# One store path less: wq's gradient of the second head block stored as whole 128-partition transfers

## The chip, the cores and the metric

The kernel runs on one core of a Trainium2 chip. The metric is the device time of one execution in microseconds; the time before is the median of three runs, 719.05 us (718.98 to 719.26). One further execution was taken with the hardware profiler and took 718.87 us; its span, from the first to the last instruction, is 717.1 us.

## The reference

The kernel computes a forward and a backward pass of one decode step: one row x of 640 values is normalised (layer norm) and goes through attention with a key and a value cache, and beside it through a gated feed-forward part. The outputs are the forward result and the gradients of x, both caches and all weights.

```python
# one token: D = 640; 32 heads of 128; caches of 8192 rows a head; F = 1728; all bf16
q = (xn @ wq), split into 32 heads
scores = einsum("bhqd,bhkd->bhqk", q, k_cache) * 128 ** -0.5
p = softmax(scores)
o = einsum("bhqk,bhkd->bhqd", p, v_cache)
A = o, heads side by side, @ wo
B = (silu(xn @ w1) * (xn @ w3)) @ w2
out = x + A + B
# and with grad_out: d x, d k_cache, d v_cache, d wq, d wo, d w1, d w3, d w2
```

The bulk is data movement: both caches (32 heads of 2 MB each, twice) are read, and gradients of the same size are written. The profile counts 151.34 MB read and 151.34 MB written. The gradient of wq, the subject here, is an outer product: row d of it is xn[d] times the gradient of q, 640 x 4096 values in bf16.

## The kernel before, in words

**Tiling.** A head's cache of 8192 x 128 values stands in SBUF as 128 partitions of 64 rows each, 16 KB a partition, so a load or store of a head moves 2 MB with one contiguous 16 KB run a partition. Heads are worked off one after another in a loop over h (L745). Four heads make a group g (its qs, do, dq and its part of wo's gradient are made together), and eight heads, two groups, make a block b of wq (GW = 8).

**A head.** DVE multiplies the cache tile by a broadcast vector (L425), PE adds up the products over identity matmuls (L427), softmax and its gradient follow on small tiles, PE makes the weighted sums over the cache (L500), and the outer products that are the caches' gradients are written into ot tiles, most rows by DVE (L451) and eight rows of every half by ACT (L445). Four ot buffers, three K buffers and two V buffers (with some early heads in borrowed tiles) carry the stream.

**Queues.** The order on every engine is written out by hand; the semaphores come from the tile framework. SP issues the loads of K and V (L116, L123) as soon as a buffer comes free, and the last two heads' stores. POOL issues the caches' gradient stores, one of 2 MB per head and cache (L458), and the stores of wq's gradient. ACT issues x, g, the wo loads and stores, and a part of the wq loads. All three queues are carried out by the same 16 DMA engines.

**wq and its gradient.** wq_two holds two blocks of wq, 128 partitions x 5 x 2 x 1024. When a group is done, finish_steps (L366) overwrites the group's part of wq_two with the gradient (L383, on ACT). After the second group of block 0 and of block 1 the block's part is stored in two pieces, WQ_PARTS = (0, 3) and (3, 2): three columns of 1024, then two. The first goes out at once through store_columns (L465), the second after the next ot store on POOL (L459 and L460). A partition's share of a piece is three or two runs of 2 KB. Once landed, the place is loaded anew with a later block of wq (L178). Block 2 and the first group of block 3 are stored late, near the end (L785), and the last group from a tile of its own (L824).

**Dealing.** store_columns issues through sparing (L145), not through one plain DMA. It cuts the 128 partitions into 120 and 8: 120 rows on 15 engines of eight rows each, so that one engine (SPARED = 4 in the kernel's own count) gets none. The 8 rows are a transfer of their own, one row on each of eight engines. `dealt` counts where the next transfer that does not use all 16 engines will begin; turn_lanes (L134) moves that place by a tiny load into lane_pad (5, 11 or 17 rows of a few bytes), which nothing reads. If the count allows, the 8 rows go ahead of the 120. At the end of the loop turn_lanes(0) puts the place back.

For block 0 and for block 1 this gives on POOL: the 120 x 3 x 1024 store, a 17-row load, the 8 x 3 x 1024 store; an ot store; the 8 x 2 x 1024 store, the 120 x 2 x 1024 store, a 17-row load. Block 0 has a 5-row load ahead of that.

Of the kernel before, what the change touches and what calls it, by code (L numbers as in the profile page):

```python
# [21 lines left out]
def kernel(  # L22
# [22 lines left out]
    nc = tc.nc  # L45
# [22 lines left out]
    WIDE = 4  # L68
    LANES = 16
    SPARED = 4  # L70
    assert H % GW == 0 and GW % GH == 0 and 0 < REST < P and P % GH == 0
    scale = float(DH) ** -0.5

# [30 lines left out]
    with tc.manual_schedule(engines=ORDERED):  # L104
# [29 lines left out]
        def turn_lanes(to):  # L134
            k = (to - dealt[0]) % LANES
            if k:
                rows = k if k > 1 else LANES + 1
                nc.gpsimd.dma_start(lane_pad[0:rows, dealt[1] % 2], wq_v[0:rows, 0:2, 0:8])
                dealt[:] = to % LANES, dealt[1] + 1

        def deal(dst, src, p0, p1):
            nc.gpsimd.dma_start(dst[p0:p1], src[p0:p1])
            dealt[0] = (dealt[0] + (LANES - 1 if p0 == 0 else P - p0)) % LANES

        def sparing(dst, src):  # L145
            rows = P - P % (LANES - 1)
            if dealt[0] == (SPARED + 1 + P - rows) % LANES:
                deal(dst, src, rows, P)
                deal(dst, src, 0, rows)
                turn_lanes(SPARED + 1)  # L150
            else:
                turn_lanes(SPARED + 1)
                deal(dst, src, 0, rows)
                turn_lanes(SPARED + 1)
                deal(dst, src, rows, P)

        def store(dst, src, later=False, by=nc.gpsimd.dma_start):
            if later:
                late.append((by, dst, src))
            else:  # L160
                by(dst, src)
# [5 lines left out]
        def wq_part(b, c0, n):  # L167
            cols = slice(b * GW * DH, (b + 1) * GW * DH)
            return wq_two[:, c0:c0 + n, b % 2, :], wq_v[:, c0:c0 + n, cols], dwq_v[:, c0:c0 + n, cols]
# [196 lines left out]
        def finish_steps(g):  # L366
            G_ = grp[g]
            wo_g = G_["wo"]
            on, on_bf = on_cols(g)
            behind_o.append((g, on_bf))  # L370
            yield
            assert not behind_o
            for r in range(GH):
                nc.scalar.activation(wo_g[:, r, :], g_bc_bf[:], ACTF.Copy, scale=on[:, r:r + 1])
            if g == NG - 2:
                store(dwo_v[g], wo_g[:], True)
            else:
                nc.scalar.dma_start(dwo_v[g], wo_g[:])
            yield
            yield  # L380
            b, k = divmod(g, HB)
            for ci in range(NC):
                nc.scalar.activation(G_["wq"][:, ci, :], G_["dqbc"][:].rearrange("p h d -> p (h d)"),  # L383
                                     ACTF.Copy, scale=xn_col[:, ci:ci + 1])
            if g < NG - HB and k == HB - 1:
                if g == NG - HB - 1:
                    part, _, dst = wq_part(b, 0, NC)
                    store(dst, part, True)
                else:
                    columns.extend((b, *part) for part in WQ_PARTS)  # L390
                    store_columns()
            if g >= NG - HB:
                store(dwq_v[:, :, g * GH * DH:(g + 1) * GH * DH], G_["wq"], True)
            grp.pop(g)
# [54 lines left out]
        def outer_v(st, vec, w2, which, h, half, n):  # L449
            j0 = half * JH  # L450
            nc.vector.tensor_tensor(st.ot[half][:, 0:n],  # L451
                                    vec.rearrange("p (a b) -> p a b", b=2).unsqueeze(1).to_broadcast([P, n, DH // 2, 2]),
                                    w2[:, j0:j0 + n, :].unsqueeze(2).to_broadcast([P, n, DH // 2, 2]), ALU.mult)
            dst = {"V": dvc, "K": dkc}[which][h]
            if h >= H - TAIL:
                nc.sync.dma_start(dst[:, j0:j0 + JH, :], st.ot[half].rearrange("p j a b -> p j (a b)"))
            elif half:
                nc.gpsimd.dma_start(dst.rearrange("p j d -> p (j d)"), st.rows[:])  # L458
                if columns:  # L459
                    store_columns()  # L460
# [4 lines left out]
        def store_columns():  # L465
            b, c0, n = columns.pop(0)
            part, _, dst = wq_part(b, c0, n)
            store(dst, part, by=sparing)

        def row_max(st):  # L470
            st.S = small.tile([P, J], F32, name="S_sb", bufs=1)
# [419 lines left out]
```

## Time and profile before

| what | value |
|---|---|
| median of three runs | 719.05 us (718.98 to 719.26) |
| profiled execution, its span | 718.87 us, 717.1 us |
| busy: PE, DVE, ACT, POOL | 557.1, 630.6, 484.2, 49.5 us (78%, 88%, 68%, 7%) |
| moved | 303.32 MB, 423 GB/s in the mean |
| stores of ot on POOL | 60 of 2048 KB, median 24.4 us from issue to landing |
| loads of K and V on SP | 32 and 32 of 2048 KB, median 26.6 and 20.0 us |
| stores of wq_two by the dealt path | 2 x 720, 2 x 48, 2 x 480, 2 x 32 KB |
| loads of lane_pad | 6, of 0.2 to 0.5 KB |

The profile's page gives busy time by engine, the span in 40 slices with the mean busy share of the 16 DMA engines and the rate, the DMA queues (q0 is POOL's, q1 is SP's, q10 is ACT's; q8 and q14 fetch instructions), the chain of work that ended last, the costliest groups of instructions, and the DMA issues with the time from issue to landing. "L458" is line 458 of the kernel. Behind the page stands the trace, which also has every DMA packet with its queue, start, length and size, and the sixteen completion counts of every transfer.

### The profile page before, as it was taken

What the parts mean: (1) busy time and instruction counts of PE and PEld (TensorE: products, weight loads), DVE (VectorE), ACT (ScalarE), POOL (GpSimd) and SP (SyncE); (2) the same over time, 40 slices, a digit from 0 to 9 for tenths busy, and PEclk for the clock granted to TensorE, in tenths of its full rate; (3) what the DMA queues carried; (4) which work ended last, traced back from release to release, by engine and by line L of the source; (5) the groups of instructions that cost most, each with busy time, mean ns of one, the idle gap of its engine ahead of it and who ended that gap; (6) DMA issues with size and microseconds to landing.
All of it is one profiled execution on the core that took longest, in us unless ns stands there. A gap on an engine that the chain in (4) does not pass through costs nothing.

```text
span 717.1 us, 9854 instructions
## 1 busy us (share of the span) xinstructions
PE 557.1 (78%) x3516; PEld 272.4 (38%) x3516; DVE 630.6 (88%) x723; ACT 484.2 (68%) x1472; POOL 49.5 (7%) x91
## 2 busy tenths in 40 slices
PE   6878988878788777776887787488868789877772
PEld 4753443334333333333343344143434334333331
DVE  5789999999989895997899899499999889899982
ACT  1275778796769656694587867468677857777552
POOL 0010000000001110000000110000000000000100
PEclk9698999998989998997899989899999878999995
DMA  9999999999999999999999999999999999999997
GB/s 364 416 425 430 431 430 430 429 429 429 428 432 428 426 428 424 429 427 426 432 431 428 430 422 426 428 430 429 428 428 431 429 430 431 429 430 429 429 421 288
DMA packets 27039, 303.32 MB, mean 423 GB/s; under 512 B 3249, under 2 KB 3959, under 8 KB 9327
## 3 DMA queue, kind: packets, MB, share of 16 engines
q1 hardware_dynamic: 12832, 154.88, 50.9%
q0 software_dynamic: 10960, 137.72, 45.2%
q10 hardware_dynamic: 3198, 10.10, 3.5%
q8 instruction: 27, 0.44, 0.2%
q14 instruction: 22, 0.17, 0.1%
HBM read 151.34 MB, written 151.34 MB: 422 GB/s over the span
## 4 chain that ended last, share of the span: by engine, by line
DMA 45%; DVE 31%; PE 17%; ACT 3%; issue 2%; POOL 0%; ACTq 0%; DVEq 0%; POOLq 0%
DMA Kt<-in_A_k_cache_dram 28%; DVE T L425 15%; DMA out_dram<-ot 12%; DVE ot L451 10%; PE ob L500 4%; DMA lane_pad<-in_A_wq_dram 4%; PE psS L427 3%; PE psDP L427 3%; ACT ot L445 2%; DVE DP_sb L526 1%; DVE S_sb L472 1%; PE dh_ps L591 1%; PE dx_ps L626 1%; PE gate_ps L602 1%; PE ps_od L516 1%
## 5 line engine op out<-in xcount | busy, mean ns | idle before, releaser
L427 PE MATMUL psDP<-T,ident_bf 128*128 128x512 bf16 x512 | 157.0, 462 | 64.6 <-DVE T L425 64.6
L427 PEld LDWEIGHTS <-ident_bf 128*128 128x128 bf16 x1024 | 108.3, 109 | 212.6 <-issue 140.1
L445 ACT ACTIVATE ot<-qs_g,Uf 128x128 bf16<-128x128 bf16 x504 | 154.0, 394 | 45.1 <-DVE Uf L539 27.2
L425 DVE TENSOR_TENSOR T<-Kt,qs_g 128x4096 bf16<-128x4096 bf16 x64 | 146.4, 2287 | 20.0 <-DMA Kt<-in_A_k_cache_dram 18.8
L445 ACT ACTIVATE ot<-do_g,Pf 128x128 bf16<-128x128 bf16 x512 | 156.3, 389 | 6.2 <-DMA out_dram<-ot 5.2
L425 DVE TENSOR_TENSOR T<-Vt,do_g 128x4096 bf16<-128x4096 bf16 x64 | 146.0, 2282 | 3.9 <-DMA Vt<-in_A_v_cache_dram 3.9
L427 PE MATMUL psS<-T,ident_bf 128*128 128x512 bf16 x512 | 129.0, 397 | 17.7 <-DVE T L425 17.7
L451 DVE TENSOR_TENSOR ot<-qs_g,U 128x3072 bf16<-128x3072 bf16 (+2 forms) x64 | 112.6, 1760 | 11.9 <-DMA out_dram<-ot 11.8
L451 DVE TENSOR_TENSOR ot<-do_g,P 128x3072 bf16<-128x3072 bf16 (+2 forms) x64 | 112.3, 1755 | 6.3 <-DMA out_dram<-ot 5.2
L458 POOL DMA_DIRECT2D out_dram<-ot x60 | 32.2, 537 | 549.2 <-DVE Uf L539 303.6
L500 PE MATMUL ob<-Vt,P 128*4 128x512 bf16 x512 | 64.1, 394 | 0.0
L500 PE MATMUL ob<-Kt,U 128*4 128x512 bf16 x512 | 60.5, 379 | 1.4 <-DVE U L533 1.4
L494 ACT ACTIVATE Pf<-E,rZ 128x16 f32<-128x16 f32 (+1 forms) x32 | 9.8, 307 | 60.2 <-DVE rZ L489 60.2
L558 ACT ACTIVATE dq_diag<-ident_bf,odq 128x128 bf16<-128x128 bf16 x32 | 12.8, 401 | 47.8 <-DVE odq L554 47.8
L516 PEld LDWEIGHTS ps_od<-pick,wide 128*128 128x128 f32 x256 | 38.1, 213 | 7.8 <-issue 3.0
L516 PE MATMUL ps_od<-pick,wide 128*128 128x2 f32 x256 | 33.8, 254 | 0.5 <-ACT wide L508 0.5
L500 PEld LDWEIGHTS <-U 128*4 128x4 bf16 x512 | 19.8, 84 | 37.5 <-DVE U L533 6.6
L476 PE MATMUL sm<-ident_f,mrow 128*128 128x128 f32 x64 | 15.9, 331 | 22.3 <-DVE mrow L474 22.3
L500 PEld LDWEIGHTS <-P 128*4 128x4 bf16 x512 | 20.8, 86 | 25.8 <-issue 3.5
L508 ACT COPY wide<-ob 128x256 f32<-128x256 f32 x64 | 20.1, 363 | 12.7 <-PE ob L500 12.7
L472 DVE TENSOR_REDUCE S_sb<-psS 128x64 f32<-128x512 f32 x32 | 21.9, 685 | 5.6 <-PE psS L427 5.6
L317 ACT COPY woT<-ps_t 128x512 bf16<-128x512 bf16 x40 | 22.9, 577 | 4.2 <-PE ps_t L312 3.6
(174 smaller groups left out, 552.4 us busy)
## 6 DMA issues: line engine op xcount, KB each, us to landing
out_dram<-ot POOLq DMA_DIRECT2D x60, 2048.0 KB, 24.4
Kt<-in_A_k_cache_dram SPq DMA_DIRECT2D x32, 2048.0 KB, 26.6
Vt<-in_A_v_cache_dram SPq DMA_DIRECT2D x32, 2048.0 KB, 20.0
out_dram<-ot SPq DMA_DIRECT2D x8, 1024.0 KB, 12.7
out_dram<-wo_g ACTq DMA_DIRECT2D x6, 640.0 KB, 15.1
wo_g<-in_A_wo_dram ACTq DMA_DIRECT2D x6, 640.0 KB, 15.8
wq_two<-in_A_wq_dram SPq DMA_DIRECT2D x1, 2560.0 KB, 23.8
w1t<-in_B_w_dram SPq DMA_DIRECT2D x1, 2160.0 KB
```

The source lines that it names most:

```text
L317: nc.scalar.copy(woT[:], ps_t[:])
L425: nc.vector.tensor_tensor(T[:], src[:, :, ds_], vec[:, ds_].unsqueeze(1).to_broadcast([P, J, DHH]), ALU.mult)
L427: nc.tensor.matmul(ps[:], lhsT=ident_bf[:], rhs=T[:, :, RUN * i:RUN * (i + 1)], start=(half == 0 and i == 0), stop=(half == 1 and i == DHH ...
L445: nc.scalar.activation(st.ot[half][:, JH - n + j].rearrange("p a b -> p (a b)"), vec, ACTF.Copy, scale=wf[:, half, j:j + 1])
L451: nc.vector.tensor_tensor(st.ot[half][:, 0:n], vec.rearrange("p (a b) -> p a b", b=2).unsqueeze(1).to_broadcast([P, n, DH // 2, 2]), w2[:, ...
L458: nc.gpsimd.dma_start(dst.rearrange("p j d -> p (j d)"), st.rows[:])
L472: nc.vector.tensor_reduce(st.S[:], st.ps["S"][:], AX.X, ALU.add)
L476: nc.tensor.matmul(st.sm[:, 8:8 + P], lhsT=mrow[:].to_broadcast([P, P]), rhs=ident_f[:], start=True, stop=True, skip_group_check=True)
L500: nc.tensor.matmul(ob[c0:c0 + WIDE, :], lhsT=w2[:, WIDE * q:WIDE * (q + 1), 0], rhs=src[:, WIDE * q:WIDE * (q + 1), :].rearrange("p j d -> ...
L508: nc.scalar.copy(part[:], ob[:, i * (WIDE // 2) * DH:(i + 1) * (WIDE // 2) * DH])
L516: nc.tensor.matmul(st.od, lhsT=st.wide[i][:, b * DH:(b + 1) * DH], rhs=pick[:, r, :], start=(r == 0), stop=(r == WIDE - 1), skip_group_che ...
L558: nc.scalar.activation(dq_diag[:], ident_bf[:], ACTF.Copy, scale=odq[:, 1:2])
```

## The change

The dealt path is kept for the blocks under SPARING_BLOCKS = 1, so for block 0. Block 1's two pieces are issued as they are, 128 partitions each, by POOL's plain dma_start. With them go the two 8-row stores and the two 17-row loads of block 1. The order on all other engines is the same.

```diff
     SPARED = 4
+    SPARING_BLOCKS = 1
...
         def store_columns():
             b, c0, n = columns.pop(0)
             part, _, dst = wq_part(b, c0, n)
-            store(dst, part, by=sparing)
+            store(dst, part, by=sparing if b < SPARING_BLOCKS else nc.gpsimd.dma_start)
```

On POOL, around the change:

```diff
 out_dram<-ot 128x8192
-out_dram<-wq_two 120x3x1024
-lane_pad<-in_A_wq_dram 17x2x8
-out_dram<-wq_two 8x3x1024
+out_dram<-wq_two 128x3x1024
 out_dram<-ot 128x8192
-out_dram<-wq_two 8x2x1024
-out_dram<-wq_two 120x2x1024
-lane_pad<-in_A_wq_dram 17x2x8
+out_dram<-wq_two 128x2x1024
 out_dram<-ot 128x8192
```

## The prediction

> **What bounds the kernel now.** I read the page's stretch by slices first, then the DMA queues, then a table of busy time by stages, then POOL's own instructions around the change, and last the packet records of the trace. The page:
>
> ```profile
> DMA  9999999999999999999999999999999999999997
> GB/s 364 416 425 430 431 430 430 429 429 429 428 432 428 426 428 424 429 427 426 432 431 428 430 422 426 428 430 429 428 428 431 429 430 431 429 430 429 429 421 288
> q1 hardware_dynamic: 12832, 154.88, 50.9%
> q0 software_dynamic: 10960, 137.72, 45.2%
> q10 hardware_dynamic: 3198, 10.10, 3.5%
> ```
>
> The mean of the 16 DMA engines is busy in every slice but the last, and the rate stays near 430 GB/s. The three queues (SP's q1, POOL's q0, ACT's q10) add up to 99.6% of 16 engines' span. By stages (time, then PE, PEld, DVE, ACT, POOL busy, granted clock, DMA share, GB/s):
>
> ```profile
> 403.00:452.00 49.00, 40.94 (x246) 19.64 (x245) 46.56 (x51) 35.49 (x110) 7.42 (x11) 0.91 1.01 425
> 452.00:470.00 18.00, 7.71 (x37) 3.70 (x35) 8.85 (x7) 6.34 (x21) 0.53 (x1) 0.72 1.02 433
> 470.00:690.00 220.00, 177.03 (x1063) 81.34 (x1064) 205.27 (x225) 160.98 (x502) 13.51 (x24) 0.91 1.01 429
> 690.00:717.10 27.10, 11.09 (x86) 6.91 (x84) 12.97 (x26) 8.13 (x22) 0.00 (x0) 0.72 0.82 334
> ```
>
> From 452 to 470 DVE is busy half the time and the DMA share is still 1.02: a stall of the compute engines costs no transfer time. Only the last stretch is not full (0.82). So the time is what the DMA engines have to carry, and the end is that of the engine that has most left. The edit is here (POOL's instructions, start and length in us, idle time before them):
>
> ```profile
> 399.88 0.53 POOL L458 DMA_DIRECT2D out_dram<-ot  x1 [7.21 <-ACT ot L445]
> 403.69 0.82 POOL L142 DMA_DIRECT2D out_dram<-wq_two  x1 [3.27 <-ACT wq_two L383]
> 404.50 0.98 POOL L138 DMA_DIRECT2D lane_pad<-in_A_wq_dram  x1
> 405.47 0.57 POOL L142 DMA_DIRECT2D out_dram<-wq_two  x1
> 412.96 0.58 POOL L458 DMA_DIRECT2D out_dram<-ot  x1 [6.92 <-issue]
> 413.54 1.33 POOL L142 DMA_DIRECT2D out_dram<-wq_two  x2
> 414.86 0.95 POOL L138 DMA_DIRECT2D lane_pad<-in_A_wq_dram  x1
> 420.54 0.58 POOL L458 DMA_DIRECT2D out_dram<-ot  x1 [4.74 <-DMA out_dram<-ot]
> ```
>
> The mean share hides which engine is last. The trace keeps start, length, size and queue of each DMA packet, not its engine. But on a full engine a packet starts 2 to 6 ns before the recorded end of the one ahead, and every full transfer gives each engine 8 rows in order; with both, the packets between 440 and 690 us fall into sixteen chains with none left over. The spared engine can be told by its marks: packets of 8 bytes where the others move 4 KB, and one of 544 bytes (a 17-row load). I call it S. Three readings:
> - S is the slow one. Its 16 KB packets between 440 and 690 took 622.9 ns on average, 282 of 379 of them over 614 ns; on the other fifteen the means are 611.1 to 614.3 ns. That is about 4.5 us lost in 250.
> - Nobody idles there: fourteen chains have at most 0.1 us of gaps, two have 0.6 and 1.2. S has none.
> - At 690 us S has 656 KB left to move before the kernel is done, the others 457 to 633 KB. At each one's pace that ends at 715.4 for S and at 707.3 to 713.9 for the rest. The last packets of the sixteen engines really end between 708.46 and 715.10 us, the second last at 714.50. So S ends the kernel, by about half a microsecond.
> The sparing shows where S stands: on POOL's queue it was 2.5 us behind the middle engine at 240 us, about level (0.3 ahead at 279) as the first block's stores ended, and 0.7 to 1.0 ahead from 465 to 480, after the second block's.
>
> **The change, part by part.** The edit touches one argument of store_columns (L468): for block 1 the two stores of wq_two go to POOL's plain issue. Built, it does that: POOL issues 128x3x1024 where it had 120 rows, 17-row load, 8 rows, and 128x2x1024 where it had 8 rows, 120 rows, 17-row load. No other engine's order moves, and block 0 and the closing turn_lanes(0) stay as they are.
> - Added on S: 8 rows of 3 + 2 pieces of 2 KB, 80 KB in 20 packets of 4 KB. Such packets took 159 ns on the other engines; on S, 2% slower, 162. 20 x 0.162 = 3.24 us.
> - Removed on S: 20 packets of 8 bytes at 9 ns (0.18), its one row of the 8x2x1024 store (0.16), two 544-byte loads at 46 ns (0.09), four completion writes at 9 ns (0.04): 0.47 us. Net 3.24 - 0.47 = +2.8 us. S is full to the end, so nothing covers it.
> - Removed on the other fifteen: eight lose a 4 KB and a 2 KB packet (0.17 + 0.08), seven a 4 KB one (0.16), all lose two 136-byte packets at 46 ns and four completions: 0.3 to 0.4 us each. Their share of the large rows stays. As they are not last, this is worth nothing; if one of them were last, 0.4 us.
> - Removed on POOL: two 8-row issues and two loads, 0.57 + 0.98 + 0.67 + 0.95 = 3.2 us of issue time. POOL sat idle 549.2 us before its 60 large stores and they land 24.4 us (median) after issue, so this is hidden; the cover would go only if the store queue ran empty, and it does not. Nobody reads lane_pad, so its waits free nothing else. Here a skill rule goes against my sum.
>
> On the pages: the Trainium skill, "DMA: Bandwidth & Descriptors", section "Rules for kernel authors", says of two transfers to disjoint partition halves that one should not bother and use one 128-partition transfer. By it the change can only gain, and the sum is rival 2's; the rows agree that the second transfer costs (0.3 to 0.4 us an engine), but the rule takes the engines as equal, which the 622.9 ns deny.
>
> - Loads and stores landing later: a transfer is done when its slowest engine is. S is behind by 2.8 us more on POOL's queue, from 0.7-1.0 ahead to about 2 behind at 465-480, where the last engine is now 2.1 behind; so little is late at first, and towards 690 the ot buffers come back about 1.4 us later (S +2.0 now, +4.8 then, the last now +3.3). DVE has 14.7 us idle in 470:690 to take it. Between 0 and 1.4 us; I take 0, since late compute does not matter while S has work queued, and it has: DVE's last work is done at 707.5, over 7 us before S ends.
>
> Sum: S ends at 715.1 + 2.8 = 717.9, the span 717.1 + 2.8 = 719.9, the profiled run 718.87 + 2.8 = 721.7. That run lies 0.18 under the median of the runs, 719.05, so I predict 719.05 + 2.8 = 721.8 us.
>
> **Rivals.**
> 1. No change: S is not last in the timed runs, or its extra work falls into slack. For: the next engine ends only 0.6 us earlier, and ten end within 5 us. Against: the extra 2.8 is larger than that 0.6, and a chain without gaps has no slack. It needs S's slowness to be a chance of this one execution; but the runs agree within 0.28 us. Time 719.05 - 0.3 = 718.7 to 719.1.
>
> On the pages: the same page, section "Latency and other measured facts", says that engines 7 and 15 are usually slower, with a guess at SWDGE's descriptor rings. Two slow engines would leave an unspared one to set the end, and the whole store would cost nothing: this rival's time. The trace shows one slow engine (the next slowest mean is 614.3), so I give that reading little.
>
> 2. Faster: the split stores jam POOL's queue, and the compute chain behind the jam sets the end. For it: the chain of waits (start and length in us) goes through that jam,
>
> ```profile
> 399.88 20.06 DMA out_dram<-ot
> 420.54 40.05 DMA out_dram<-ot
> ```
>
> and in the list of waits (us in all, times, longest) DVE and ACT wait on landings of ot:
>
> ```profile
> DVE ot L451 <- DMA out_dram<-ot: 17.1, 3, 9.9
> ACT ot L445 <- DMA out_dram<-ot: 15.4, 3, 9.1
> ```
>
> A landing of 40.05 us where 24.4 is usual. If POOL's 3.2 us came off that chain and reached the end, 719.05 - 3.2 = 715.8. It decides only if DMA engines fall idle while compute stalls; the 452:470 row says they don't.
> 3. Slower by more: the later buffers (1.4 us) do hold back compute until S's queue runs dry near the end: 721.8 + 1.4 = 723.2.
> That the change doesn't do what it says is ruled out by the built order.
>
> **How the numbers follow.** My case, 720.6 to 722.8: 0.72. Rival 1: 0.12. Rival 2: 0.05. Rival 3: 0.11. From no change to 0.2% (1.4 us) is about what a measurement of this kernel can tell. Faster by over 0.2%: 0.05; within: 0.12; slower: 0.72 + 0.11 = 0.83. The range runs from 719.3, leaving out rivals 1 and 2 (0.17), to 723.4, which takes in rival 3.
>
> **What would show it.** In the profile after: no lane_pad load and no 8-row store between 403 and 420; DMA share still 1.01 in the stretches to 690; the GB/s of the last slice lower, since fifteen engines wait for one; the last landings (out_dram<-dwq_t, wo_g) some 2.8 us later against the first of their sixteen increments, which spread 7.2 us now (708.7 to 715.9); S without 8-byte packets after block 0, and last by about 3 us. I am wrong if the engine that ends last is not S, if S shows gaps, or if ot landings in the 420 to 460 stretch fall from 40 us and the end moves forward with them.

## The result and the profile after

| | median | runs |
|---|---|---|
| before | 719.01 us | 718.48 to 719.71, six runs |
| after | 721.14 us | 720.63 to 722.51, six runs |

The ratio is 1.0033 (95% interval 1.0020 to 1.0046): slower by 2.4 us, 1.4 to 3.3. The profiled run of after is the longest of its six (722.51 us, span 720.7; the spans of the other five are 718.9 to 719.9), so its trace shows the step somewhat larger than it mostly is.

The page of after, its DMA slices and two of its queues:

```profile
DMA  9999999999999999999999999999999999999995
GB/s 367 413 430 426 430 433 428 429 430 428 430 431 429 429 427 423 431 426 426 432 430 426 429 427 429 429 426 425 430 428 429 428 430 430 425 431 429 428 408 217
q1 hardware_dynamic: 12832, 154.88, 50.7%
q0 software_dynamic: 10816, 137.72, 44.9%
```

The page of before ended 421 288; after ends 408 217, and the last slice's busy share falls from 7 tenths to 5. POOL's queue has 144 packets less (10816 for 10960) and the same bytes. Nothing was added to the work. By stages (time, busy time of PE, PEld, DVE, ACT, POOL, granted clock, DMA share, GB/s):

```profile
403.00:452.00 49.00, 42.26 (x251) 19.39 (x253) 45.97 (x51) 36.92 (x112) 4.20 (x7) 0.91 1.01 428
452.00:470.00 18.00, 9.21 (x48) 4.46 (x45) 11.43 (x11) 6.93 (x23) 0.53 (x1) 0.72 1.02 432
470.00:690.00 220.00, 169.40 (x1029) 78.90 (x1033) 200.41 (x216) 159.33 (x496) 13.52 (x24) 0.92 1.01 428
690.00:717.10 27.10, 15.72 (x101) 9.78 (x100) 15.68 (x31) 9.14 (x25) 0.00 (x0) 0.69 0.82 332
717.10:720.70 3.60, 0.00 (x0) 0.00 (x0) 0.00 (x0) 0.00 (x0) 0.00 (x0) 0.50 0.04 13
```

Up to 690 the share is 1.01 to 1.02, as it was before, and from there to 717.1 it is the same 0.82. Within that last stretch it is lower than before for a while: 0.93 from 694 to 698 and from 702 to 706, where before had 1.00 and 1.02, so some engines ran short of work there. What is plainest is the new last row: 3.6 us in which no compute engine works and the DMA share is 0.04. The end of after, microsecond by microsecond, says what that is:

```profile
714.00:715.00 1.00, 0.00 (x0) 0.00 (x0) 0.00 (x0) 0.00 (x0) 0.00 (x0) 0.50 0.23 71
715.00:716.00 1.00, 0.00 (x0) 0.00 (x0) 0.00 (x0) 0.00 (x0) 0.00 (x0) 0.50 0.05 20
716.00:717.00 1.00, 0.00 (x0) 0.00 (x0) 0.00 (x0) 0.00 (x0) 0.00 (x0) 0.50 0.07 28
717.00:718.00 1.00, 0.00 (x0) 0.00 (x0) 0.00 (x0) 0.00 (x0) 0.00 (x0) 0.50 0.06 25
718.00:719.00 1.00, 0.00 (x0) 0.00 (x0) 0.00 (x0) 0.00 (x0) 0.00 (x0) 0.50 0.07 23
```

A share of 0.06 is 1/16: one engine alone is at work from 715 to 719. In before these rows read 0.10 and 0.01 for 714 to 716, and nothing behind. Read as chains of packets, as in the prediction, that engine ends at 719.12 us and the next at 715.08; in before the two ended at 715.10 and 714.50. The last engine's 16 KB packets take 625.4 ns on average (256 of 358 over 614 ns), the other fifteen 611.5 to 615.4 ns; it has no idle time, and at 674 us it has 1136 KB left where the others have 896 to 1040. At its pace 1136 KB are 44.4 us, and it ends 45.1 us later, so it was not among those that ran short. No engine has a packet of 8 bytes between 290 and 680 us; before had 36 of them from 410 to 450. The last engine is S, which now carries block 1's rows.

POOL around the change, in after:

```profile
400.61 0.53 POOL L459 DMA_DIRECT2D out_dram<-ot  x1 [7.21 <-ACT ot L446]
405.07 0.76 POOL L162 DMA_DIRECT2D out_dram<-wq_two  x1 [3.93 <-DVE rZ L490]
412.25 0.56 POOL L459 DMA_DIRECT2D out_dram<-ot  x1 [6.43 <-issue]
412.81 0.72 POOL L162 DMA_DIRECT2D out_dram<-wq_two  x1
419.11 0.56 POOL L459 DMA_DIRECT2D out_dram<-ot  x1 [5.58 <-ACT ot L446]
```

Two issues in place of six; POOL's busy time falls from 49.5 to 46.3 us and the end does not move with it. The jam of rival 2 stays (chain of waits, then waits for landings of ot):

```profile
419.11 38.97 DMA out_dram<-ot
```

```profile
DVE ot L452 <- DMA out_dram<-ot: 15.4, 3, 8.1
ACT ot L446 <- DMA out_dram<-ot: 13.7, 3, 7.2
```

The landing took 40.05 us and takes 38.97, and the two waits fall from 32.5 to 29.1 us together. Compute got more done there (DVE is busy 11.43 us in 452 to 470, not 8.85), and the kernel is slower all the same.

### The profile page after: what moved, and what is told of

Same layout as the page of the kernel before. It is cut to its first block, busy times and chain, and to the rows that moved or that the text cites. A ratio compares the mean times of both kernels' runs of the same rounds, so it can differ in the third digit from the quotient of the medians.

```text
span 720.7 us, 9833 instructions
## 1 busy us (share of the span) xinstructions
PE 552.3 (77%) x3500; PEld 272.4 (38%) x3516; DVE 630.3 (87%) x723; ACT 484.5 (67%) x1472; POOL 46.3 (6%) x87
## 3 DMA queue, kind: packets, MB, share of 16 engines
q0 software_dynamic: 10816, 137.72, 44.9%
## 4 chain that ended last, share of the span: by engine, by line
DMA 46%; DVE 30%; PE 17%; ACT 4%; issue 1%; POOL 0%; ACTq 0%; DVEq 0%; POOLq 0%
DMA Kt<-in_A_k_cache_dram 32%; DVE T L426 15%; DMA out_dram<-ot 9%; DVE ot L452 9%; PE ob L501 5%; DMA lane_pad<-in_A_wq_dram 4%; PE psS L428 3%; ACT ot L446 2%; PE psDP L428 2%; DVE DP_sb L527 1%; PE dx_ps L627 1%; DVE S_sb L473 1%; PE dh_ps L592 1%; PE gate_ps L603 1%; DVE P L492 1%
## 5 line engine op out<-in xcount | busy, mean ns | idle before, releaser
L426 DVE TENSOR_TENSOR T<-Kt,qs_g 128x4096 bf16<-128x4096 bf16 x64 | 146.3, 2287 | 24.5 <-DMA Kt<-in_A_k_cache_dram 23.2
```

Source lines behind the costliest of these rows:

```text
L426: nc.vector.tensor_tensor(T[:], src[:, :, ds_], vec[:, ds_].unsqueeze(1).to_broadcast([P, J, DHH]), ALU.mult)
```

## The experiments

Each was timed against the kernel before on the same chip; a ratio is to that kernel.

**How much of S's spared work is put back, and on which engine.** Four kernels.

```diff
 # other_engine: block 1 stays dealt, but past engine 12 of the kernel's count
-            store(dst, part, by=sparing)
+            store(dst, part, by=lambda d, s: sparing(d, s, SPARED if b == 0 else OTHER))
 # spare_none: the changed kernel with block 0 whole too
-    SPARING_BLOCKS = 1
+    SPARING_BLOCKS = 0
 # three_whole: only block 1's piece of three columns is stored whole
-            store(dst, part, by=sparing)
+            store(dst, part, by=nc.gpsimd.dma_start if b and n == 3 else sparing)
 # halves: the changed kernel, block 1's pieces in partitions 0-63 and 64-127
+                store(dst[0:P // 2], part[0:P // 2]); store(dst[P // 2:P], part[P // 2:P])
```

> The dealt path stays for both blocks, but block 1 spares engine 12 of the kernel's count in place of engine 4 (S). Theory, S carries the end: S gets its eight rows of both pieces back and 4 KB of an 8-row store, as in the change, so the time is 721.1 to 722.0 us, 2.1 to 3.0 over before. Rival, the form of the stores costs it (whole transfers of 2 KB runs, their place in POOL's queue): the form is that of before, so 719.0 us.

> Block 0 is stored whole too. Theory: S carries another 80 KB, so the step of the change comes twice, 4.2 us by the measured 2.1 and 5.6 by the predicted 2.8: 723.2 to 724.6 us. Rival, the place in the run counts (block 1's stores meet a jam that block 0's don't): the time stays within 1 us of the changed kernel, 720.1 to 722.1. A third view, that the loads into lane_pad in block 0 with POOL's wait of 12.3 us for one of them cost time, would make it faster than the changed kernel, under 721.

> Only block 1's piece of three columns is stored whole, the piece of two is still dealt: S carries 48 KB more than before, not 80. Theory: 48/80 of the step, 1.3 us by the measured 2.1, 1.7 by the predicted 2.8: 720.3 to 720.7 us. Rival, form and place: no share is given by it; all of the step or none, 721.1 or 719.0.

> The change, with each of block 1's two pieces cut into partitions 0 to 63 and 64 to 127: twice the transfers, the same bytes on every engine, no load between. Theory: as the change, 721.1 us, 0.3 more or less. Rival, fewer or larger transfers are what moves the time: away from 721.1 by 0.7 or more, back towards 719.0.

| kernel | early KB put back on S | median | ratio (95%) |
|---|---|---|---|
| three_whole | 48 | 720.31 us | 1.0021 (1.0012 to 1.0029) |
| the change | 80 | 721.14 us | 1.0033 (1.0020 to 1.0046) |
| halves | 80 | 721.21 us | 1.0036 (1.0024 to 1.0048) |
| other_engine | 80 | 721.97 us | 1.0041 (1.0029 to 1.0054) |
| spare_none | 160 | 724.14 us | 1.0072 (1.0058 to 1.0085) |

The time follows the bytes given back to S: 1.5, 2.4 and 5.2 us for 48, 80 and 160 KB, 0.030 to 0.033 us per KB (the prediction's 2.8 us for 80 KB is 0.035). It doesn't follow the form of the store: halves has two stores a piece and no tiny load, the change has one, and they agree. The weightiest run is other_engine. It has the cut, the loads and as many POOL issues as before (in another order), and costs as much as the change, within the intervals. The packet records say why. In other_engine, chains of packets from 428 to 500 us:

```
                            16 KB packets   over 614 ns   4 KB store packets   544-byte loads
engine without rows         614.0 ns        5 of 108      0                    2
the slow engine             622.6 ns        68 of 104     15                   0
the other fourteen          611 to 617 ns   1 to 5 each   14 to 17             0
```

The engine that is spared is an ordinary one, and the slow one keeps its rows. The end looks like that of after, other_engine:

```profile
715.00:716.00 1.00, 0.00 (x0) 0.00 (x0) 0.00 (x0) 0.00 (x0) 0.00 (x0) 0.50 0.05 19
716.00:717.00 1.00, 0.00 (x0) 0.00 (x0) 0.00 (x0) 0.00 (x0) 0.00 (x0) 0.50 0.06 26
717.00:718.00 1.00, 0.00 (x0) 0.00 (x0) 0.00 (x0) 0.00 (x0) 0.00 (x0) 0.50 0.06 26
```

and in spare_none the lone engine goes on to 720.74 us:

```profile
717.00:718.00 1.00, 0.00 (x0) 0.00 (x0) 0.00 (x0) 0.00 (x0) 0.00 (x0) 0.50 0.06 27
718.00:719.00 1.00, 0.00 (x0) 0.00 (x0) 0.00 (x0) 0.00 (x0) 0.00 (x0) 0.50 0.07 27
719.00:720.00 1.00, 0.00 (x0) 0.00 (x0) 0.00 (x0) 0.00 (x0) 0.00 (x0) 0.50 0.06 26
```

The sixteen completion counts, one from each engine, show the lone engine without any chaining. Of the store of dwq_t (the last group's part of wq's gradient, stored near the end), in the profiled execution of each kernel:

| kernel | fifteenth count | sixteenth count | apart |
|---|---|---|---|
| before | 715.56 us | 715.87 us | 0.3 us |
| three_whole | 715.21 | 716.46 | 1.2 |
| halves | 716.38 | 718.01 | 1.6 |
| other_engine | 716.14 | 718.98 | 2.8 |
| the change | 715.45 | 719.48 | 4.0 |
| spare_none | 716.52 | 721.10 | 4.6 |

The fifteenth count moves by 1.3 us in all, the sixteenth by 5.2. Each row is one execution: that of three_whole is the fastest of its eleven, that of the change the longest of its six.

**Sparing S late.** If the step is S's sum, it can be taken back by dealing block 2's store past S as well, which is issued near the end. All four kernels of this kind missed what the theory expected.

```diff
 # late_relief (on the changed kernel), spare_three (on the kernel before)
-                    store(dst, part, True)
+                    store(dst, part, True, by=sparing)
 # late_cols (on the kernel before): the same in two pieces of three and two columns
+                    for c0, n in WQ_PARTS:
+                        part, _, dst = wq_part(b, c0, n)
+                        store(dst, part, True, by=sparing)
 # late_split (on the kernel before): 120 and 8 partitions, no 17-row load between
+                    store(dst, part, True, by=split)
```

> The changed kernel, with block 2's late store of 1280 KB dealt past S: S gets back 80 KB some 260 us after it took them on. Theory: only S's sum counts, so the step is undone, 718.7 to 719.3 us, though block 1's stores are whole as in the change. Rival, form and place of block 1's stores: 721.1 us as the change, or more for the extra transfers.

> Before, with block 2's late store dealt past S as well: S carries 80 KB less. Theory: S would end 2.8 us earlier, at 712.3, but the next engines end at 714.1 to 714.5 and get 0.2 to 0.4 more, so the gain is cut to 0.2 to 0.6 us: 718.4 to 718.8 us. A full gain of 2.1 to 2.8 (716.4) would say that S sets the pace of the whole run and not only the end.

> The kernel before, with block 2's late store dealt past S in pieces of three and two columns (the form of the stores of blocks 0 and 1, 120x3 and 120x2 rows), not in one piece of five (600 rows). In the two runs that dealt it in one piece the rate fell from 424 to 350 to 370 GB/s between 690 and 700 us at a busy share of 1.00, and they came out 2.6 us too long. If it was that form which slowed the packets: the rate stays at 420 and S, spared 3.2 us, ends before the rest, 718.4 to 718.9 us. If it is dealing a store beside the stores that SP issues at that time, whatever its form: the rate falls again to 350 to 380 and the time is 720.9 to 722.

> The kernel before, with block 2's late store in two parts of 120 and 8 partitions and no tiny load between them: the 120 partitions go over the fifteen engines without S, as the cursor stands, and the 8 partitions start on S, which keeps one eighth of them, 5 rows of 2 KB, 0.4 us, in place of 3.2. If the tiny load of 17 rows slowed the packets of the two earlier runs: the rate stays at 420 GB/s and the time is 718.4 to 719.0 us. If it is the two parts: the rate falls again, and the time is 720.9 to 722.

Measured: late_relief 721.41 us, 1.0037 (1.0024 to 1.0049); spare_three 721.64, 1.0042 (1.0030 to 1.0054); late_cols 722.11, 1.0049 (1.0034 to 1.0063); late_split 722.00, 1.0037 (1.0025 to 1.0049). The table by stages shows what undid the gain. First three_whole, where this store is issued whole, then spare_three:

```profile
680.00:690.00 10.00, 7.57 (x40) 3.92 (x40) 9.44 (x12) 6.81 (x23) 0.00 (x0) 0.83 1.00 419
690.00:700.00 10.00, 7.42 (x67) 4.02 (x65) 8.68 (x11) 5.11 (x17) 0.00 (x0) 1.00 1.02 424
700.00:708.00 8.00, 4.11 (x21) 3.08 (x21) 4.70 (x17) 3.43 (x7) 0.00 (x0) 0.65 1.01 420
```

```profile
680.00:690.00 10.00, 7.56 (x42) 3.44 (x40) 9.65 (x13) 6.79 (x23) 0.00 (x0) 0.83 1.00 367
690.00:700.00 10.00, 7.43 (x67) 4.03 (x65) 8.68 (x11) 5.13 (x17) 0.00 (x0) 1.00 1.00 351
700.00:708.00 8.00, 4.13 (x22) 3.09 (x21) 4.71 (x17) 3.43 (x7) 0.00 (x0) 0.61 1.02 407
```

The engines are as busy (1.00 to 1.02) and move less: 10.4 MB in these 28 us for 11.8, and the 1.35 MB missing are 3.2 us at 420 GB/s. That is the whole distance from 718.4, the lower end of what was expected, to the 721.64 measured. The packets of every queue are longer there: from 684 to 705 us in spare_three the store's 4 KB packets take 200 ns on average (median 159), and from 682 to 703 SP's 8 KB packets of ot 345 ns (median 309, the longest 1560). late_relief has 371 GB/s in 690 to 700, late_cols 349 and late_split 364, all at a share of 1.00 to 1.01. So it is not the one piece of 600 rows alone (late_cols), nor the 17-row load (late_split); what the four share is a store cut in 120 and 8 partitions beside SP's stores. The same cut at 405 to 452 us, beside loads, leaves the rate at 425. What slows the packets is open: the trace has a packet's length, not the reason for it. Whether S was relieved can't be seen under this loss, so these four tell nothing for or against S, except that a late deal is no way to help it.

**Loading one engine.** The kernel before, with the first 17 rows of block 1's second piece stored a second time (the same data to the same place), all on one engine: S, or engine 6.

```diff
+                if b == 1 and n == 2:
+                    back = dealt[0]; turn_lanes(4)          # ballast_6: turn_lanes(6)
+                    nc.gpsimd.dma_start(dst[0:LANES + 1], part[0:LANES + 1])
+                    dealt[0] = 5; turn_lanes(back)          # ballast_6: 7
```

> Before, with both blocks dealt, and one more store behind block 1's second piece: 17 rows of it, 68 KB, once more to the same place with the same data, all on S. Nothing waits for it but the next load into that half of wq_two. Theory: 17 packets of 4 KB at 162 ns are 2.8 us more on S, so 721.1 to 721.8 us. Rival: 68 KB of 303 MB are nothing, 719.0 us.

> The same 68 KB store, on engine 6 of the kernel's count in place of S. Theory: engine 6 is one of those that end some microseconds ahead of S (I estimate 3 to 6 from the ends of 708.5 to 714.5), so the 2.7 us (17 packets at 159 ns) stay in its slack: 718.8 to 719.6 us. Rival, any extra transfer in POOL's queue at this place costs: as ballast_s, 721 us or more.

Measured: ballast_s 727.29 us, 1.0129 (1.0106 to 1.0153); ballast_6 725.11, 1.0088 (1.0075 to 1.0101). Both are far above what was expected, in the main for one reason. POOL in ballast_6:

```profile
413.71 0.95 POOL L138 DMA_DIRECT2D lane_pad<-in_A_wq_dram  x1
433.73 0.95 POOL L138 DMA_DIRECT2D lane_pad<-in_A_wq_dram  x1 [19.07 <-DMA lane_pad<-in_A_wq_dram]
452.24 0.95 POOL L472 DMA_DIRECT2D out_dram<-wq_two  x1 [17.56 <-DMA out_dram<-wq_two]
453.19 0.57 POOL L138 DMA_DIRECT2D lane_pad<-in_A_wq_dram  x1
453.75 2.17 POOL L458 DMA_DIRECT2D out_dram<-ot  x4
```

The extra turn waited 19.07 us for a free lane_pad, the second store of the same rows 17.56 us for the first to land, and four stores of ot stood behind them, the first for some 33 us (it is issued at 420.54 in before). By then the stream had run dry:

```profile
450.00:452.00 2.00, 2.00 (x21) 0.92 (x18) 1.72 (x3) 2.00 (x6) 0.00 (x0) 1.00 0.35 105
452.00:454.00 2.00, 2.00 (x14) 0.73 (x14) 0.00 (x0) 0.65 (x1) 1.76 (x3) 1.00 0.98 181
```

By 500 us ballast_6 had moved 2.0 MB less than before, which is 4.6 us at 429 GB/s, of the 6.5 us that it lost; the rest was not traced. Both kernels have that loss (ballast_s has 0.37 and 184 GB/s in those two stretches, and 1.9 MB less at 500 us), so only their difference speaks: 2.2 us by the medians, 0.0041 of 718.65 = 2.9 us by the ratios, for 68 KB on S and not on engine 6. The expectations stood 2.3 us apart. The two intervals just do not meet (1.0101 and 1.0106). The packet records show the 68 KB where they were meant to be: 17 packets of 4 KB, most of them back to back on one engine, in ballast_s on the slow one (110 of its 207 16 KB packets from 463 to 600 us took over 614 ns), in ballast_6 on an ordinary one (17 of 209). The ends differ in the same way: the sixteenth count of dwq_t comes 5.4 us after the fifteenth in ballast_s and 1.7 us in ballast_6.

**Sparing S once in mid-kernel.** The changed kernel with one store of ot (head 21, K) dealt, past engine 4 and, as a control, past engine 12.

```diff
-                nc.gpsimd.dma_start(dst.rearrange("p j d -> p (j d)"), st.rows[:])
+                if h == 21 and which == "K":
+                    sparing(dst.rearrange("p j d -> p (j d)"), st.rows[:])   # relief_ot12: spared=12
+                else:
+                    nc.gpsimd.dma_start(dst.rearrange("p j d -> p (j d)"), st.rows[:])
```

> The changed kernel, with one more edit: one gradient of K of 2 MB (head 21, stored by POOL in mid-kernel, a row of 16 KB for each partition) is stored in parts of 120 and 8 partitions past engine 4, so that S is spared 8 packets of 16 KB, 8 x 0.625 = 5.0 us, and eight of the others take one more each, 0.61 us. Theory (the step of the change is the 3.2 us of packets that it gave back to S): S ends at 719.1 - 5.0 = 714.1 and no longer last; the next engine, which ended at 715.1, ends at 715.1 to 715.7; the step is undone but for 0 to 0.6 us: 719.0 to 719.7 us. Rival (the step comes from the whole form of the two stores, or from when they land, at 400 to 450 us): nothing is undone there, 721.1 or above. Second rival (a dealt transfer slows the packets around it, as the late one did in two earlier runs): the granted rate falls for some 10 us around the dealt store, 721 to 723.

> As the run before it, but the store of head 21 is dealt past engine 12 in place of engine 4. Same form, same place, same number of instructions; only the engine that is spared is another. Theory (S's sum sets the end): nothing is undone, and S may be among the eight that take one more packet of 16 KB: 721.1 to 721.8 us. Rival (dealing a store there helps whichever engine it spares): 719.0 to 719.7.

Measured: relief_ot 723.44 us (721.78 to 726.85), 1.0068 (1.0049 to 1.0087); relief_ot12 722.02, 1.0041 (1.0028 to 1.0054). The control came out 0.2 us above its range, relief_ot 4 us above. The profile of relief_ot is that of its longest run, 726.85 us. Its packet chains from 503 to 543 us:

```
                        16 KB packets   over 614 ns   rows of the dealt store
engine without rows     642.0 ns        6 of 59       0
the slow engine         690.6 ns        25 of 56      8
17-row load falls on a third engine
```

So the edit did not do what its expectation takes for granted: an ordinary engine went without rows, and the slow one had all eight. In the dealt stores of wq_two, with rows of 4 and 6 KB, the 17-row load falls on the engine without rows, as the kernel's count has it; with rows of 16 KB it does so in neither run, so the count does not hold for them (why, the runs don't show). The engine that ends relief_ot is alone from 718 on and ends at 723.31:

```profile
716.00:718.00 2.00, 0.00 (x0) 0.00 (x0) 0.00 (x0) 0.00 (x0) 0.00 (x0) 0.50 0.09 32
718.00:720.00 2.00, 0.00 (x0) 0.00 (x0) 0.00 (x0) 0.00 (x0) 0.00 (x0) 0.50 0.07 28
720.00:722.00 2.00, 0.00 (x0) 0.00 (x0) 0.00 (x0) 0.00 (x0) 0.00 (x0) 0.50 0.06 25
```

The rate also fell for a time after the dealt store (relief_ot):

```profile
540.00:545.00 5.00, 4.75 (x36) 2.54 (x35) 4.96 (x5) 3.85 (x11) 0.04 (x1) 0.80 0.95 401
545.00:550.00 5.00, 4.04 (x28) 1.53 (x26) 3.65 (x5) 4.31 (x13) 0.49 (x1) 1.00 1.00 364
```

where relief_ot12 has 433 and 429 GB/s. The dealt store itself had landed by 539.0 us. The long packets from 545 to 550 are those of SP's loads, 839 ns on average beside 612 for POOL's stores, and SP had just issued a V load at 544.72 us; so this looks like the first loads after a pause, as in the two ballasts, and not like the cut, which no run separates. That a relief of S in mid-kernel takes the step back was thus never shown. That the step comes with the work of S, and not with the form of the stores, was shown: by other_engine, and by the difference of the two ballasts.

## Why the prediction was right

The forecast was 721.8 us; the median of after is 721.14, within the range, and the step is 2.1 us by the medians and 2.4 by the ratio where 2.8 was predicted, inside the ratio's interval.

- **DMA engines bound the kernel, a stall of compute costs no transfer time.** Held: the share is 1.01 to 1.02 in every stretch to 690, and DVE got 2.6 us more done between 452 and 470 with nothing gained at the end. By 690 that lead is gone: since 403 DVE has worked 257.8 us, in before 260.7.
- **S is slow and ends last.** Held, and it is the trace's plainest sign: one engine alone for 4 us, the one with the long packets. How slow it was differs between the two traces, however: 622.9 ns in before, 625.4 in after, with the rest near 612. That is 2.5 ns on some 400 packets, about 1 us, and may be part of why the profiled run of after is 3.6 us above that of before and its median only 2.1 above.
- **Added and removed on S, net 2.8 us.** The right term, sized a little high if at all: 0.030 to 0.033 us per KB over three doses where it had 0.035.
- **The other fifteen's gain of 0.3 to 0.4 us is worth nothing.** Fits, and can't be checked by itself: the second last engine ended at 714.50 and ends at 715.08.
- **POOL's 3.2 us of issue time are hidden.** Held: 49.5 to 46.3 us busy, and halves, with two issues more than the change, comes out alike.
- **Later buffers cost nothing.** The price held: rival 3's 723.2 us lies above the interval, which ends at 722.3. The lateness itself was larger in this trace than the 1.4 us reckoned: DVE's waits for K grow from 18.8 to 23.2 us, and its last work is done at 711.2 us where it was done at 707.5. It cost nothing of its own because S still has 7.9 us of work behind that, as the prediction had argued.
- **Rival 1** is out by the interval, which starts at 1.0020. **Rival 2** had its mechanism half right: the jam eased, 40.05 to 38.97 us, and the end moved the other way.
- **What would show it.** The landings of the last store of dwq_t spread from 711.7 to 719.5 us, 7.8 for 7.2 before: less than "2.8 us more against the first", because the first landing came 3.0 us later too. The better sign is the sixteenth landing against the fifteenth: 4.0 us for 0.3. S last by about 3 us: by 4.0 in this run.

On the pages: the Trainium skill, "DMA: Bandwidth & Descriptors", section "Rules for kernel authors", advises one 128-partition transfer over two on disjoint halves. For even halves the runs find no difference (721.21 and 721.14 us), and carried over to the uneven cut that leaves out the slow engine, of which the rule does not speak, it would be wrong by 2.4 us here. The Trainium skill, in the same page's section "Latency and other measured facts", expects two slow engines, 7 and 15; every trace that was followed here, five of them, has one, and the packets don't say which number it has.

## What to carry to other kernels

When the mean DMA share is full to the end, ask which of the sixteen engines ends last: its own sum of packets is the time, and moving 80 KB off it was worth 2.4 us here while 80 KB off another was worth nothing. Look at the last microseconds of the span in steps of one: a share that stays at 1/16 is one engine working alone. And deal such work out early, in a form that is known to land where it is counted: the same cut near the end, or with larger rows, cost time where it should have saved some.

## What the runs showed of the hardware

- A busy share of 1.00 is not a full rate: with a cut store beside SP's stores the sixteen engines moved 349 to 371 GB/s at that share, for 424 without it. The cause is open.
- After the stream had run dry (share 0.35 for 2 us), the first 16 KB loads took 1.0 to 1.8 us each, 181 GB/s at a share of 0.98, before they fell back to about 611 ns (ballast_6).
- One engine was slower than the other fifteen in every profile that was followed, at much the same pace: 622 to 625 ns a 16 KB packet in four of them. In relief_ot the mean from 503 to 674 us is 637, but that holds the 690.6 ns around the dealt store; from 553 to 674 it is 622.9.
- A store of 120 rows of 16 KB left out another engine than a count by rows says, while rows of 4 and 6 KB followed it.
